# Retention and a GELU layer on one core: a hand-written order of the chunked retention, queries loaded four tokens a partition, and the second layer by seven half-size products

## The chip, the cores and the metric

The kernel runs on one core of one Trainium2 chip. The metric is the device time of a launch in microseconds (us), the median of several executions. An execution called fast is one whose time lies within 1.5% of the fastest of its kernel; a single execution on one core has the state "unknown". The executions of the kernel before lay between 359.5 and 362.5 us on all occasions, so a difference of one us between two single executions means nothing.

The engines are written as the profile has them: PE multiplies matrices (PEld loads its weights), DVE, ACT and POOL are the vector, scalar and general engines, SP issues most DMAs.

## The reference, cut to what matters

```python
# q, k, v: [8 batches, 8 heads, 576 tokens, 64], float32
scores = (q @ k.transpose(0, 1, 3, 2)) / sqrt(64)
gamma  = 1.0 - 2.0 ** (-5.0 - arange(8))                 # one decay a head
Dmat   = where(rel >= 0, gamma[:, None, None] ** rel, 0.0)   # rel = query position - key position
attn   = (scores * Dmat) @ v
x      = attn.transpose(0, 2, 1, 3).reshape(4608, 512)
h      = x @ w_in                                        # w_in  [512, 2048]
g      = gelu_tanh(h)
out    = g @ w_out                                       # w_out [2048, 512], out [4608, 512] float32
```

Because the decay is a power, both kernels fold it into q and k (one factor a token and a head), cut a batch into four chunks of 128 tokens and a tail of 64, and carry a 64 x 64 state a head from chunk to chunk. The work of PE is then mostly the two layers.

## The kernel before

The two layers go in 9 blocks of 512 tokens, numbered 0 to 8. In block t the 16 steps `up` are the first layer and the 8 steps `down` the second; between them stand the steps of the attention of batch t+1. Attention of batch 0 comes before block 0. Only PE's order is written by hand. Some lines are joined here, and the comments are added.

```python
    def load_batch(b):                       # 64 floats (256 B) to a piece, for q, k and v alike
        ...
                nc.sync.dma_start(
                    out=t.rearrange("p (h d) -> p h d", d=D),
                    in_=src[b, :, 128 * c : 128 * c + 128, :].rearrange("h s d -> s h d"),
                )
    ...
    def tr_pair(b, p):                       # q and k of two heads are turned on PE, 8 transposes
        ...
        s = sb.tile([128, 1024], F16, tag="qk", name="qk", bufs=6)
        nc.vector.tensor_copy(out=s, in_=t)
    ...
    def state_scan(b):                       # the states are copied by ACT
        ...
                nc.scalar.copy(out=td[r, c, :, r], in_=w[r])
    ...
    def ffn_steps(t):
        def up(fc):
            hp = bank("hp", 2, "hp")
            for ct in range(4):
                nc.tensor.matmul(hp, w_in_sb[:, ct, 128 * fc : 128 * fc + 128],
                                 xT[:, ct, TB * t : TB * t + TB], start=(ct == 0), stop=(ct == 3))
            nc.scalar.activation(out=gT[:, fc, :], in_=hp, func=AF.Gelu_apprx_tanh)
        def down(i, half):                   # 64 matmuls of 512 columns a block
            if half == 0:
                op[i] = bank("att", 6, "op")
            for f in range(8 * half, 8 * half + 8):
                nc.tensor.matmul(op[i], gT[:, f, 128 * i : 128 * i + 128], w_out_sb[:, f, :],
                                 start=(f == 0), stop=(f == NF - 1))
            ...
    slots = {1: 0, 2: 1, 3: 2, 5: 3, 7: 4, 8: 5, 11: 6, 14: 7, 16: 8, 19: 9}
    with tc.manual_schedule(engines={PE}):
        load_batch(0)
        cast_batch(0, {"k": nc.vector, "q": nc.gpsimd, "v": nc.gpsimd})
        for g in range(4):
            load_w_in(g)
        load_batch(1)                        # batch 1 is loaded ahead of w_out
        ...
        for f in range(NF):
            load_w_out(f)
        for f in range(NF):
            cast_w_out(f)
        for t in range(NTB):
            ...
                cast_batch(t + 1, {"k": nc.gpsimd, "q": nc.vector, "v": nc.gpsimd})
                steps = att_steps(t + 1)
            ...
            for i, f in enumerate(ffn_steps(t)):
                f()
                if i in slots and slots[i] < len(steps):
                    steps[slots[i]]()
```

## Time and profile before

| | before |
|---|---|
| median time | 362.1 us (360.08 to 362.14, 3 runs) |
| span of the profiled execution | 358.8 us |
| start of block 1 | 86.9 us |
| length of blocks 1 to 6 | 35.5, 35.1, 35.1, 35.9, 35.5, 35.5 us |
| length of block 7 | 27.6 us |
| start of block 8 to the end | 31.6 us |

The first view is the page of the kernel before: the span, the busy time of each engine, and two rows of digits, where each digit is a fortieth of the span (about 9 us), in tenths.

```profile
span 358.8 us, 6008 instructions
PE 316.4 (88%) x2400; PEld 159.1 (44%) x2400; DVE 125.9 (35%) x269; ACT 161.9 (45%) x303; POOL 70.3 (20%) x101
PE   0176368799999999999999999999999999999995
DMA  9979989994692898598937931100110011011012
```

PE is full from the tenth slice on. Before that PE is not full and the DMA engines are. The same is told in us by the windows view; its columns are the stretch, its length, then busy time and count of PE, PEld, DVE, ACT and POOL, the granted clock of PE, the DMA share, and GB/s.

```profile
0.00:30.00 30.00, 9.39 (x118) 6.62 (x118) 17.59 (x65) 6.06 (x12) 15.39 (x31) 0.96 0.99 220
30.00:57.00 27.00, 16.71 (x138) 8.86 (x139) 10.94 (x22) 11.97 (x22) 7.58 (x10) 0.66 1.00 243
157.50:192.60 35.10, 34.54 (x285) 17.57 (x284) 14.99 (x29) 17.32 (x33) 10.30 (x15) 1.00 0.76 168
```

The last row is block 3: PE is busy 34.5 of 35.1 us, DVE 15.0. The timeline of PE shows the marks of the block structure; its columns are start, length, engine, line, operation, written tile, read tiles, shapes, count, and in brackets the idle time just before and what ended it.

```profile
71.64 1.89 PE L369 MATMUL op<-w_out_sb,gT 128*128 128x512 f16 x8
...
86.90 1.89 PE L355 MATMUL hp<-xT,w_in_sb 128*128 128x512 f16 x8
...
138.41 1.89 PE L355 MATMUL hp<-xT,w_in_sb 128*128 128x512 f16 x8 [0.44 <-ACT gT L361]
```

L355 is `up`, L369 is `down`. Block 0's second layer begins at 71.64 us, block 1 at 86.90, and in a later block PE idles no longer than 0.44 us at a time.

### The profile page before, as it was taken

Reading aid. Unit: us, or ns where it says so; the run is one execution under the profiler, and the core shown is the slowest. Engines: PE = TensorE matmul, PEld = TensorE weight load, DVE = VectorE, ACT = ScalarE, POOL = GpSimd, SP = SyncE. Lnnn points to the kernel's source line nnn. Section 1 sums busy time; section 2 is a strip of 40 time slices with the busy share of each in tenths; the row PEclk is TensorE's granted clock in tenths of the full one; section 3 lists DMA queues with packets and bytes.
Section 4 is the critical chain, followed back from the end, with each engine's and each line's share of the span. In section 5 each row is a group of like instructions: output and inputs, shape, how many; then the busy total and the mean of one; then the engine's idle time right before and its main releaser. Section 6 shows DMA issues by size and latency. Waiting matters only on the chain.

```text
span 358.8 us, 6008 instructions
## 1 busy us (share of the span) xinstructions
PE 316.4 (88%) x2400; PEld 159.1 (44%) x2400; DVE 125.9 (35%) x269; ACT 161.9 (45%) x303; POOL 70.3 (20%) x101
## 2 busy tenths in 40 slices
PE   0176368799999999999999999999999999999995
PEld 0153134344544454455445544554454444444442
DVE  5287238430762174227422771172117200000000
ACT  1037318722682268236723662366236624714721
POOL 8610430342051333232321232000000000000000
PEclk9995669899999999999999999999999999999999
DMA  9979989994692898598937931100110011011012
GB/s 173 205 230 319 224 193 360 219 188 134 144 218 81 194 225 163 127 235 170 194 108 187 216 82 58 58 2 2 58 60 0 2 60 58 0 60 59 0 38 79
DMA packets 122715, 46.52 MB, mean 130 GB/s; under 512 B 113984, under 2 KB 113984, under 8 KB 122688
## 3 DMA queue, kind: packets, MB, share of 16 engines
q1 hardware_dynamic: 122688, 46.15, 55.2%
q8 instruction: 18, 0.29, 0.4%
q14 instruction: 9, 0.07, 0.1%
HBM read 36.70 MB, written 9.44 MB: 129 GB/s over the span
## 4 chain that ended last, share of the span: by engine, by line
PE 67%; ACT 10%; DMA 9%; DVE 7%; SPq 4%; issue 1%; POOL 1%; DVEq 0%; ACTq 0%
PE op L369 35%; PE hp L355 24%; DVE ret L246 4%; ACT gT L361 4%; SPq L118 3%; DMA ld<-in_moe_w_out_dram 3%; DMA ld<-in_q_dram 3%; ACT tbd_128 L281 2%; ACT tbd_130 L281 2%; PE xs L290 2%; DMA ld<-in_moe_w_in_dram 2%; PE xs L308 2%; PE st L221 2%; PE tr L189 2%; DVE ws L278 1%; DMA ld<-in_v_dram 1%
## 5 line engine op out<-in xcount | busy, mean ns | idle before, releaser
L355 PE MATMUL hp<-xT,w_in_sb 128*128 128x512 f16 x576 | 141.6, 388 | 7.7 <-ACT gT L361 7.5
L369 PE MATMUL op<-w_out_sb,gT 128*128 128x512 f16 x576 | 128.1, 379 | 0.0
L361 ACT ACTIVATE gT<-hp 128x512 f16<-128x512 f32 x144 | 85.2, 598 | 58.6 <-PE hp L355 57.9
L355 PEld LDWEIGHTS <-w_in_sb 128*128 128x128 f16 x576 | 54.7, 99 | 68.8 <-issue 16.7
L369 PEld LDWEIGHTS <-gT 128*128 128x128 f16 x576 | 55.6, 98 | 65.3
L377 ACT COPY ost<-op 128x512 f32<-128x512 f32 x36 | 21.1, 586 | 100.9 <-PE op L369 66.0
L246 DVE TENSOR_TENSOR ret<-st,cm 128x512 f16<-128x512 f32 x64 | 40.7, 684 | 49.5 <-PE st L221 49.4
L146 POOL TENSOR_TENSOR ck<-ld,sc 128x512 f16<-128x512 f32 (+1 forms) x35 | 34.8, 997 | 82.2 <-DMA ld<-in_k_dram 60.9
L195 DVE COPY qk<-tr 128x1024 f16<-128x1024 f16 x32 | 21.9, 686 | 56.5 <-PE tr L189 56.5
L146 DVE TENSOR_TENSOR cq<-ld,sc 128x512 f16<-128x512 f32 (+1 forms) x35 | 22.6, 660 | 40.2 <-DMA ld<-in_q_dram 40.2
L142 POOL CAST cv<-ld 128x512 f16<-128x512 f32 (+1 forms) x40 | 23.1, 590 | 67.4 <-DMA ld<-in_v_dram 36.8
L189 PE MATMUL tr<-ident,ck 128*128 128x128 f16 x128 | 14.7, 234 | 23.5 <-DVE ck L146 15.0
L189 PEld LDWEIGHTS <-ck 128*128 128x128 f16 x128 | 10.6, 104 | 31.7 <-DVE ck L146 15.5
L325 ACT CAST xT<-xs 128x512 f16<-128x512 f32 x32 | 17.2, 589 | 5.0 <-PE xs L308 4.9
L189 PE MATMUL tr<-ident,cq 128*128 128x128 f16 x128 | 14.2, 236 | 1.2 <-POOL cq L146 1.0
L281 ACT CAST tbd_128<-ws 64x256 f16<-64x256 f32 x32 | 12.9, 403 | 3.1 <-DVE ws L278 2.6
L281 ACT CAST tbd_130<-ws 64x256 f16<-64x256 f32 x32 | 12.9, 403 | 2.4 <-DVE ws L278 2.0
L171 ACT CAST w_in_sb<-ld 128x512 f16<-128x512 f32 x8 | 5.0, 620 | 19.6 <-DMA ld<-in_moe_w_in_dram 19.5
L290 PE MATMUL xs<-ret,cv 128*64 128x128 f16 x256 | 11.3, 227 | 1.3 <-DVE ret L246 1.0
L278 DVE TENSOR_TENSOR ws<-vs,gt 128x256 f32<-128x256 f32 x24 | 11.8, 492 | 1.4
L221 PE MATMUL st<-qk 64*128 64x128 f16 x256 | 11.9, 226 | 0.3 <-DVE qk L195 0.3
L221 PEld LDWEIGHTS <-qk 64*128 64x128 f16 x256 | 7.6, 98 | 9.8 <-issue 7.4
(56 smaller groups left out, 125.7 us busy)
## 6 DMA issues: line engine op xcount, KB each, us to landing
out_dram<-ost SPq DMA_DIRECT2D x36, 256.0 KB, 2.0
ld<-in_k_dram SPq DMA_DIRECT2D x32, 256.0 KB, 4.8
ld<-in_q_dram SPq DMA_DIRECT2D x32, 256.0 KB, 4.9
ld<-in_v_dram SPq DMA_DIRECT2D x32, 256.0 KB, 4.9
ld<-in_moe_w_in_dram SPq DMA_DIRECT2D x16, 256.0 KB, 6.4
ld<-in_moe_w_out_dram SPq DMA_DIRECT2D x16, 256.0 KB, 6.0
ld<-in_k_dram SPq DMA_DIRECT2D x16, 64.0 KB, 3.3
ld<-in_q_dram SPq DMA_DIRECT2D x16, 64.0 KB, 2.6
```

Source lines behind the costliest of these rows:

```text
L142: eng[key].tensor_copy(out=dst, in_=raw)
L146: eng[key].tensor_tensor(out=dst.rearrange("p (h d) -> p h d", d=D), in0=raw.rearrange("p (h d) -> p h d", d=D), in1=sc[:, s0 : s0 + nh].u ...
L189: nc.tensor.transpose(t[:, 512 * i + 128 * c : 512 * i + 128 * c + 128], a[key][:, 512 * c + 128 * p : 512 * c + 128 * p + 128], ident,)
L195: nc.vector.tensor_copy(out=s, in_=t)
L221: nc.tensor.matmul(st[hl][:, 128 * c : 128 * c + 128], qk[r, 128 * c : 128 * c + 128], qk[r, 512 + 128 * c : 512 + 128 * c + 128], start=T ...
L246: nc.vector.tensor_tensor(out=r, in0=st[:, 0:w], in1=m.rearrange("p c i -> p (c i)"), op=ALU.mult)
L281: nc.scalar.copy(out=td[r, c, :, r], in_=w[r])
L290: nc.tensor.matmul(x[64 * hl : 64 * hl + 64, 128 * c : 128 * c + 128], a["v"][:, col(c, p, hl)], a["ret", p, hl][:, 128 * c : 128 * c + 12 ...
L355: nc.tensor.matmul(hp, w_in_sb[:, ct, 128 * fc : 128 * fc + 128], xT[:, ct, TB * t : TB * t + TB], start=(ct == 0), stop=(ct == 3),)
L361: nc.scalar.activation(out=gT[:, fc, :], in_=hp, func=AF.Gelu_apprx_tanh)
L369: nc.tensor.matmul(op[i], gT[:, f, 128 * i : 128 * i + 128], w_out_sb[:, f, :], start=(f == 0), stop=(f == NF - 1),)
L377: nc.scalar.copy(out=o, in_=op[i])
```

## The change

The intent was threefold. First, less work on PE: the second layer of blocks 1 to 8 becomes seven products of sums of blocks (112 matmuls of 256 columns in place of 64 of 512), and the transposes of q and k for batches 4 to 7 go to the DMA engines. Second, a shorter opening: q is loaded four tokens to a partition, in pieces of 1 KB in place of 256 B, and both weights are loaded before batch 1. Third, the order of every engine, not of PE alone, is written by hand. The sums of weights that the seven products need are made once, on POOL and DVE: half of them in the second layer of block 0, half in block 1. The sums of activations are made in every block by DVE.

The diff, cut to its core (`...` marks cuts, the comments are added; the loads, the decay factors, the chunked attention and the order of the opening are rewritten too):

```diff
+    elif key == "q":                        # 4 tokens a partition: 1 KB pieces
+            nc.sync.dma_start(
+                out=t.rearrange("p (h x) -> p h x", h=2),
+                in_=src[b, 2 * c : 2 * c + 2, 0:M0, :].rearrange("h (p j) d -> p h (j d)", j=QT),
+            )
...
+    seq += [("i", g, ct) for g in range(4) for ct in range(4)]     # w_in, then w_out, then batches 1 to 7
+    seq += [("o", f) for f in range(NF)]
+    for b in range(1, B):
...
+    def weight_sums(f):
+        s = slice(f, f + 2)
+        d, w = (sb.tile([128, 2, HD], F32, tag=n, name=n, bufs=b) for n, b in (("wd", 2), ("we", 1)))
+        nc.vector.tensor_tensor(out=wt["1"][:, s], in0=W12[:, s], in1=W11[:, s], op=ALU.subtract)
+        nc.gpsimd.tensor_tensor(out=d, in0=W22[:, s], in1=W12[:, s], op=ALU.subtract)
+        nc.gpsimd.tensor_tensor(out=wt["2"][:, s], in0=d, in1=W11[:, s], op=ALU.add)
+        nc.gpsimd.tensor_tensor(out=w, in0=W21[:, s], in1=W11[:, s], op=ALU.subtract)
+        nc.gpsimd.tensor_tensor(out=wt["4"][:, s], in0=w, in1=d, op=ALU.subtract)
...
+    def act_sums(t, f0, f1):                # 4 calls a block
+        nc.vector.tensor_tensor(out=s["1"], in0=a21, in1=a22, op=ALU.add)
+        nc.vector.tensor_tensor(out=s["2"], in0=s["1"], in1=a11, op=ALU.subtract)
+        nc.vector.tensor_tensor(out=a21, in0=a11, in1=a21, op=ALU.subtract)
+        nc.vector.tensor_tensor(out=s["4"], in0=a12, in1=s["2"], op=ALU.subtract)
...
+    def prod(t, m, u):                      # m: one of 7 products, u: one of 2 halves
+        for f in range(NH):
+            nc.tensor.matmul(
+                op[tag][:, HD * u : HD * u + HD], lhs(f), rhs[:, f],
+                start=(new and u == 0 and f == 0), stop=(f == NH - 1), skip_group_check=True,
+            )
...
+    at(0, 2, lambda: turn_pe(1, "q", 0, 8, A.copy))      # block 0, steps 2 and 4 of its second layer
+    at(0, 4, lambda: turn_pe(1, "q", 8, 8, V.tensor_copy))
...
+    for n in range(4):
+        at(*((0, 30), (0, 32), (1, 3), (1, 6))[n], lambda n=n: weight_sums(2 * n))
+        at(1, (1, 2, 12, 14)[n], lambda n=n: weight_copy(2 * n))
+    for b in range(2, B):
...
+        if b == 2:
+            t0, eng = 1, {"k": V, "q": P, "v": A}
+        elif b == 3:                         # batch 3's casts stand in block 1 as well
+            ut = [9, 10, 11, 12] + [14, 15, 16, 17, 18, 19, 20, 21] + [22, 22, 22]
+            t0, eng = 1, {"k": P, "q": P, "v": A}
...
+        if b >= NPE:                         # NPE = 4: batches 4 to 7
+            at(t0, ut[-1] + 1, lambda b=b: turn_dma(b))
...
+        slots = {2: (6, 10, 15, 19, 25)}.get(b, (1, 7, 12, 19, 25))
...
-        def down(i, half):
-            ...
-                    gT[:, f, 128 * i : 128 * i + 128],
-                    w_out_sb[:, f, :],
```

`at(t, u, f)` puts work after step u of block t, on every engine.

## The prediction

> **What bounds the kernel now.** Three parts, from the timeline of PE.
>
> 1. Opening, 0 to 86.9 us, where the second block of 512 tokens starts. Loads rule it: the windows show DMA busy 0.99 (0–30 us) and 1.00 (30–57 us), PE busy only 9.4 and 16.7 us there. Loads in 256 B pieces (q, k, v) move 173–205 GB/s, the 2 KB pieces of the weights 319–360. [...] w_out is loaded behind batch 1 and lands near 62 us, so block 0's second layer starts only at 71.6 us.
> 2. Blocks 1 to 6 with attention of the next batch: 35.5 us each, PE-bound. 128 matmuls of 512 columns at 216 ns (13.8 us for 64, chain of waits) are 27.65 us; attention is the other 7.8 us: 36 transposes at 56 ns = 2.0 us, scores 1.4, states 0.6, value products 1.3, state products 0.8, the rest waits (for GELU 7.5 us in the whole run).
> 3. Blocks 7 and 8 without attention: 27.65 us each, PE-bound, then 3.8 us of last copy and store.
>
> **What the change does.**
>
> - Second layer of blocks 1–8: 112 matmuls of 256 columns in place of 64 of 512. At 216/2 plus about 1 ns (an estimate; transposes with their own weight loads hold 56 ns for 128), 12.2 us for 13.8: −1.6 us a block, −12.7 us, all on PE and so on the path. Added: 16 DVE sums of activations (about 0.4 us each) and five adds of products (0.65): 10 us a block on an engine busy 15 of 34. Not on the path.
> - Batches 4–7: transposes of q and k leave PE for DMA: −2.0 us a block, and −1 us more from a finer interleaving. The moved 1.2 MB must land within some 12 steps (about 13 us). [...] At 200 GB/s they take 6 us: hidden.
> - State copies move from ACT to DVE, casts to POOL and ACT. Attention per block: about 7.0 us for batches 2 and 3, 4.9 for 4–7, in place of 7.8: −13 us over six blocks.
> - Opening: q in 1 KB pieces (3 us a batch instead of 5.5), weights both before batch 1. Batch 0 landed by 19 us, w_in 31, w_out 43, batch 1 60, then 3–4 us of attention: block 1 starts near 64 us instead of 86.9: −23 us.
> - Fillers, sums of weights on POOL (17 us, needed near 84 us): no time.
>
> Sum: 64 + 2×33.3 + 4×31.2 + 2×26.2 + 3.7 = 311.5 span, plus 3.3 (362.1 against the profile's 358.8), plus 1–2 us new waits: **316 us, 308 to 329** (8 in 10). Chances: faster by over 2% 0.97, within 0.02, slower 0.01.
>
> **What would show it.** In the timeline of PE: block 1 starts at 61–68 us; blocks 3–6 last 31 us and blocks 1–2 33; blocks 7–8 26.2; product matmuls 109 ns start to start. DMA share 0.9 or more until 60 us. DVE about 22 us a block, still below PE.
>
> **What would make it wrong.** Transposes by DMA slower than their window, or their issue holding ACT so that GELU and then PE wait; 256-column matmuls not holding 109 ns; DVE late with sums or with the adds that free the product banks; three attention banks too few, so that PE waits for DVE; opening gated by POOL's 16 weight casts rather than by DMA.

No term of the sum went with them: it stays at 311.5 us of span and 316 us of time. Three figures in it are estimates. The 3 us for a batch's queries: four loads of 256 KB are 1.05 MB, 2.9 us at the 360 GB/s that the page before shows for the pieces of 2 KB; no 1 KB piece was in that trace. In the trace after, the windows 60:62 and 62:64, in which batch 2's queries load and its keys and values begin, show 291 and 297 GB/s. The 200 GB/s for the transposes by DMA is what the page before shows for loads in 256 B pieces; what the transposes took is told under e11. The 0.4 and 0.65 us of DVE's additions and adds of products came out as 0.42 to 0.43 us where POOL did not slow them, and as 0.687.

## The result, and the profile after

The kernel after takes 344.07 us (median of 4 runs, 343.66 to 344.59), the one before beside it 361.63 (360.08 to 362.14, 4 runs). The ratio of the two is 0.9531, with a 95% interval from 0.9503 to 0.9559. A ratio is the mean time of one kernel's fast runs over that of the other's of the same rounds, so it is not quite the ratio of the medians. The direction was right. The size was not: 17.6 us came in place of 46, and the time lies above the range of 308 to 329.

```profile
span 342.3 us, 6651 instructions
PE 310.2 (91%) x2660; PEld 189.1 (55%) x2660; DVE 213.1 (62%) x437; ACT 170.9 (50%) x274; POOL 108.8 (32%) x129
PE   5869849994697999999999999999999999999995
DVE  7751644879978467757976677467546752442432
POOL 7748234999920460039224404100000000000000
PEclk9999969997889999999999999999999999999999
```

In the tenth and eleventh slice (77 to 94 us) PE is down to 4 and 6 tenths and its clock to 7 and 8, while DVE and POOL are both full. That is block 1, as the windows show beside the loading of the weights and a later block:

```profile
25.00:40.00 15.00, 14.55 (x78) 6.42 (x78) 5.41 (x11) 9.03 (x17) 9.72 (x14) 1.00 1.02 368
71.50:104.00 32.50, 24.08 (x184) 11.85 (x181) 28.30 (x39) 16.44 (x29) 24.21 (x21) 0.84 0.69 157
154.60:187.40 32.80, 32.12 (x299) 20.31 (x297) 25.35 (x46) 17.70 (x28) 15.94 (x17) 1.00 0.84 194
```

In the second row DVE is busy 28.3 us for 39 instructions (0.73 us each); in the third, 25.4 us for 46 (0.55 each). The waits of PE in block 1, from its timeline:

```profile
71.45 2.79 PE L390 MATMUL hp<-xT,w_in_sb 128*128 128x512 f16 x12
...
83.52 0.61 PE L289 MATMUL st<-tq,tk 64*128 64x128 f16 x8 [4.70 <-DVE tk L254]
...
84.42 4.78 PE L390 MATMUL hp<-xT,w_in_sb 128*128 128x512 f16 x12
...
93.95 0.40 PE L289 MATMUL st<-tq,tk 64*128 64x128 f16 x8 [3.21 <-DVE tk L254]
...
94.52 4.45 PE L390 MATMUL hp<-xT,w_in_sb 128*128 128x512 f16 x12
```

PE waits 4.70 and 3.21 us for DVE's copy of the turned keys (`tk`), and after each wait the same 12 matmuls that took 2.79 us at 71.45 take 4.78 and 4.45. The granted clock of this stretch is 0.84 (second row of the windows), so here each of the two waits costs its own length and 2.0 or 1.7 us more. The length of a wait alone does not tell: after one of 2.28 us 12 matmuls took 4.45 us (e13_mended3), and after one of 2.79 us they took 2.76 (e11_all_pe_turns), as in stretches with a clock of 1.00. What sets the clock was not shown. With three smaller waits the waits of block 1 are 9.9 us; the slow stretches add about 4.0 (2.0 and 1.7 for the two rows of 12, the rest from the small groups between them, an estimate from the same timeline).

Blocks 3 to 6 and the products look like this. In the first fence are two rows of PE from block 3 and one of ACT; in the second, products of block 7.

```profile
168.15 1.29 ACT L377 CAST xT<-xs 128x512 f16<-128x512 f32 x1
168.41 0.40 PE L289 MATMUL st<-tq,tk 64*128 64x128 f16 x8
169.49 0.32 PE L309 MATMUL us<-cv,ck 128*64 128x64 f16 x8 [0.68 <-ACT xT L377]
```

```profile
299.61 1.91 PE L466 MATMUL opA<-w_out_sb,gT 128*128 128x256 f16 x16
301.36 1.91 PE L466 MATMUL opB<-wt,s 128*128 128x256 f16 x16
```

Sixteen product matmuls start 1.75 us apart, so 109 ns each, as predicted. The wait of 0.68 us recurs in each of blocks 3 to 6: PE wants a bank which ACT's copy of the attention output has not yet freed.

Where the time went, by stage of the span:

| stage | before | predicted | after | after − before | after − predicted |
|---|---|---|---|---|---|
| start of block 1 | 86.90 | 64 | 71.45 | −15.45 | +7.45 |
| block 1 | 35.47 | 33.3 | 49.46 | +13.99 | +16.16 |
| block 2 | 35.12 | 33.3 | 33.65 | −1.47 | +0.35 |
| blocks 3 to 6, sum | 142.06 | 124.8 | 131.21 | −10.85 | +6.41 |
| block 7 | 27.62 | 26.2 | 26.07 | −1.55 | −0.13 |
| block 8 and end | 31.63 | 29.9 | 30.46 | −1.17 | +0.56 |
| span | 358.8 | 311.5 | 342.3 | −16.5 | +30.8 |

Three rows carry the miss of 30.8 us in the span: block 1 with half of it, the opening, and blocks 3 to 6. The predicted time had another 3.3 us between the span and the time, where 1.9 were found, and 1 to 2 us for new waits, which are in the rows here.

### The profile page after: what moved, and what is told of

Same layout as the page of the kernel before. It is cut to its first block, busy times and chain, and to the rows that moved or that the text cites. A ratio compares the mean times of both kernels' runs of the same rounds, so it can differ in the third digit from the quotient of the medians.

```text
span 342.3 us, 6651 instructions
## 1 busy us (share of the span) xinstructions
PE 310.2 (91%) x2660; PEld 189.1 (55%) x2660; DVE 213.1 (62%) x437; ACT 170.9 (50%) x274; POOL 108.8 (32%) x129
## 4 chain that ended last, share of the span: by engine, by line
PE 72%; DMA 8%; DVE 8%; SPq 5%; ACT 4%; issue 1%; POOL 1%; DVEq 0%
PE hp L390 30%; PE opB L466 12%; PE opC L466 9%; PE opA L466 8%; PE op L408 3%; DMA ld<-in_moe_w_in_dram 3%; DMA ld<-in_moe_w_out_dram 3%; PE xs L338 3%; SPq L90 3%; PE st L289 2%; PE xs L356 2%; ACT xT L377 2%; PE us L309 2%; DMA ld<-in_q_dram 2%; SPq L78 1%
## 5 line engine op out<-in xcount | busy, mean ns | idle before, releaser
L377 ACT CAST xT<-xs 128x512 f16<-128x512 f32 x31 | 40.1, 1294 | 29.5 <-PE xs L356 22.6
L223 POOL TENSOR_TENSOR cq<-ld,sc 128x512 f16<-128x512 f32 x28 | 31.6, 1155 | 46.0 <-DMA tq<-cq 21.0
L232 POOL TENSOR_TENSOR ck<-ld,sc 128x512 f16<-128x512 f32 x27 | 28.9, 1089 | 37.3 <-PE us L309 29.6
L466 PEld LDWEIGHTS <-s 128*128 128x128 f16 x384 | 36.5, 98 | 4.9
L466 PE MATMUL opA<-w_out_sb,gT 128*128 128x256 f16 x256 | 30.9, 273 | 0.0
L329 DVE CAST tbd<-ws 64x256 f16<-64x256 f32 x48 | 20.6, 430 | 1.2
L408 PE MATMUL op<-w_out_sb,gT 128*128 128x512 f16 x64 | 17.7, 396 | 0.5 <-ACT ost L413 0.5
L219 ACT CAST cv<-ld 128x512 f16<-128x512 f32 x28 | 17.5, 628 | 1.1 <-DMA ld<-in_v_dram 1.1
L466 PE MATMUL opB<-wt,gT 128*128 128x256 f16 x128 | 16.4, 273 | 0.5 <-DVE ost L480 0.5
L449 DVE TENSOR_TENSOR s<-s,gT 128x512 f16<-128x512 f16 x32 | 15.9, 498 | 1.1
```

What stands on the lines that cost most here:

```text
L223: eng.tensor_tensor(out=dst.rearrange("p (j l d) -> p l j d", j=QT, l=2), in0=raw.rearrange("p (l j d) -> p l j d", l=2, j=QT), in1=sc[:, ...
L232: eng.tensor_tensor(out=dst.rearrange("p (h d) -> p h d", d=D), in0=raw.rearrange("p (h d) -> p h d", d=D), in1=sc[:, s0 : s0 + nh].unsque ...
L329: cp(out=td[r, c, :, r], in_=w[r])
L377: nc.scalar.copy(out=xT[:, g0 : g0 + 2].rearrange("p g n (i j) -> p g n j i", j=QT), in_=src)
L408: nc.tensor.matmul(op[i], gT[t][:, f, i], w_out_sb[:, f, :], start=(f == 0), stop=(f == NF - 1))
L466: nc.tensor.matmul(op[tag][:, HD * u : HD * u + HD], lhs(f), rhs[:, f], start=(new and u == 0 and f == 0), stop=(f == NH - 1), skip_group_ ...
```

## The experiments

Thirteen kernels ran. Those of one look are single executions (state unknown) and are read by their blocks. The first four were compared with one run of the kernel before on the same chip, 360.58 us, those named e5 to e8 with one of 359.91, and e11 with six fast ones (median 360.9). e9, e10, e12 and e13 were timed (four fast executions each, the median is given); their blocks, as those of the kernel after, are from one profiled execution of 342.38, 335.29, 333.95, 330.62 and 344.22 us.

| run | us | start of block 1 | block 1 | block 2 | blocks 3 to 6, typical |
|---|---|---|---|---|---|
| after | 344.07 | 71.45 | 49.46 | 33.65 | 32.80 |
| e1_no_sums | 338.03 | 70.92 | 43.81 | 33.65 | 32.80 |
| e2_memsets | 340.54 | 72.27 | 44.95 | 33.65 | 32.80 |
| e3_late_q | 344.70 | 70.09 | 51.14 | 33.65 | 32.80 |
| e4_plain | 353.80 | 73.88 | 40.05 | 35.93 | 35.27 |
| e5_early_sums | 342.35 | 77.11 | 41.95 | 33.65 | 32.80 |
| e6_keys_act | 346.58 | 71.07 | 47.75 | 36.11 | 32.80 |
| e7_slots | 341.75 | 72.18 | 49.01 | 33.12 | 32.26 |
| e8_before_split | 362.16 | 85.76 | 35.75 | 35.98 | 35.42 |
| e9_combined | 344.69 | 75.99 | 43.17 | 35.82 | 32.25 |
| e10_mended | 333.58 | 75.16 | 38.96 | 33.98 | 32.26 |
| e11_all_pe_turns | 351.09 | 73.10 | 47.69 | 34.55 | 34.55 |
| e12_mended2 | 333.99 | 67.43 | 46.14 | 33.13 | 32.26 |
| e13_mended3 | 329.74 | 67.30 | 42.16 | 33.98 | 32.26 |

The theory of the first runs for block 1: while POOL reads its operands, DVE's additions with two inputs in SBUF wait for it. DVE's instructions stand in the written order in the trace, so the cast and the copy of the keys behind the additions come late, PE waits for the keys, and its clock falls (to 0.84 over the stretch). The rival: DVE simply has too much to do in block 1, whatever POOL does.

The ground for the theory is how DVE's and POOL's timelines of the kernel after lie together (DVE's rows, then POOL's):

```profile
77.62 1.26 DVE L449 TENSOR_TENSOR s<-s,gT 128x512 f16<-128x512 f16 x1
78.80 1.48 DVE L450 TENSOR_TENSOR gT<-gT 128x512 f16<-128x512 f16 x1
80.20 1.37 DVE L451 TENSOR_TENSOR s<-gT,s 128x512 f16<-128x512 f16 x1
...
85.99 1.79 DVE L329 CAST tbd<-ws 64x256 f16<-64x256 f32 x2
...
96.49 0.59 DVE L329 CAST tbd<-ws 64x256 f16<-64x256 f32 x2
...
97.57 0.43 DVE L449 TENSOR_TENSOR s<-s,gT 128x512 f16<-128x512 f16 x1
```

```profile
77.26 1.33 POOL L432 TENSOR_TENSOR we<-w_out_sb 128x512 f32<-128x512 f16 x1
78.68 1.32 POOL L433 TENSOR_TENSOR wt<-we,wd 128x512 f16<-128x512 f32 x1
79.96 1.33 POOL L430 TENSOR_TENSOR wd<-w_out_sb 128x512 f32<-128x512 f16 x1
```

The addition of L449 takes 0.43 us at 97.57, alone, and 1.26 at 77.62. Each of the three long additions ends 0.28 to 0.29 us after the POOL instruction that ran when it began (78.88 after 78.59, 80.28 after 80.00, 81.57 after 81.29): in these three cases DVE's addition lasted until a POOL instruction had ended. The masking of the scores has one input in PSUM, and its mean is 684 ns before and 685 after. The state copies (`tbd`), which the change moved from ACT to DVE, have one input, in SBUF, and are held up too: two of them take 1.79 us at 85.99, beside POOL's casts, and 0.59 at 96.49, with POOL idle.

### e1_no_sums: POOL's sums of weights left out (wrong result)

```diff
-        nc.gpsimd.tensor_tensor(out=d, in0=W22[:, s], in1=W12[:, s], op=ALU.subtract)
-        (and the three other POOL sums)
+    (wt["2"], wt["4"] set once to 0.02; weight_copy copies wt["1"])
```

> The 16 sums of weights on POOL are left out (constants in their place, so the result is wrong on purpose); casts, DVE work and PE order stay. Theory, POOL's work on SBUF holds up DVE in block 1: the adds of activations on DVE in block 1 fall from 1.2-1.5 us to 0.42-0.6, the waits of PE for the key copies (4.7 and 3.2 us) go to under 1 us each, block 1 lasts 34-37 us instead of 49.5, the run about 330-333 instead of 344. Rival, DVE simply has more work of its own in block 1 than it can do: nothing changes, 343-345.

Measured: 338.03 us; block 1 43.81 us in place of 49.46; the first wait for `tk` 0.41 us in place of 4.70. The second stayed:

```profile
86.85 0.61 PE L289 MATMUL st<-tq,tk 64*128 64x128 f16 x8 [3.28 <-DVE tk L254]
```

So the sums of weights cost 5.65 us of block 1, about a third of its 16 us over the prediction, and the run missed its expectation. For the first wait the rival is out, since DVE does the same instructions here. In the same trace DVE's four additions took 0.42 us each from 76 to 78 us, with POOL idle; from 81 to 86, where POOL cast batch 3's queries, two state copies took 1.89 us in place of 0.59 and two of the four additions 1.16 and 1.27. POOL has more than one job in block 1, and the second one did what the first had done.

### e2_memsets: as many POOL instructions, which only write (wrong result)

```diff
-        (the four POOL sums)
+        w = sb.tile([128, 1200], F32, tag="we", name="we", bufs=1)
+        for _ in range(4):
+            nc.gpsimd.memset(w, 0.0)
```

> As e1, but POOL stays as busy as in the changed kernel: in the place of each sum a memset of a scratch tile that takes about the same 1.25 us and reads nothing. Theory, DVE waits only for POOL operations that read SBUF: as e1, 330-333. Rival, any POOL operation holds DVE up, or POOL's full queue delays the casts behind it: block 1 stays near 49 us and the run near 344.

Measured: 340.54 us, block 1 44.95 us, waits for `tk` 0.40 and 4.98: neither the 330 to 333 of the theory nor the 49 us block of the rival. One trace holds both cases. POOL's rows come first, then DVE's:

```profile
73.32 9.18 POOL L431 MEMSET we<- 128x1200 f32 x8
82.47 4.55 POOL L223 TENSOR_TENSOR cq<-ld,sc 128x512 f16<-128x512 f32 x4
```

```profile
77.94 0.42 DVE L446 TENSOR_TENSOR s<-s,gT 128x512 f16<-128x512 f16 x1
...
84.94 1.16 DVE L446 TENSOR_TENSOR s<-s,gT 128x512 f16<-128x512 f16 x1
```

Beside memsets the same line takes 0.42 us, beside the casts 1.16. In this trace a busy POOL did not slow the additions by itself (0.42 to 0.43 us for the four beside memsets); a POOL that reads SBUF did (1.16 to 1.27 for the four beside the casts). By what the two get in each other's way was not shown. The second wait is longer than in e1 (4.98 us for 3.28): POOL reaches batch 3's casts only after the memsets, and all four additions fall beside them.

### e3_late_q: batch 1's queries turned later in block 0

The kernel after has its other long wait in the opening (PE's timeline):

```profile
47.05 0.61 PE L248 MATMUL tr<-ident,cq 128*128 128x128 f16 x4 [5.16 <-DVE cq L223]
```

Step 2 of block 0's second layer puts transposes of batch 1's queries in front of matmuls, some of whose weights had already landed.

```diff
-    at(0, 2, lambda: turn_pe(1, "q", 0, 8, A.copy))
-    at(0, 4, lambda: turn_pe(1, "q", 8, 8, V.tensor_copy))
+    at(0, 14, lambda: turn_pe(1, "q", 0, 8, A.copy))
+    at(0, 15, lambda: turn_pe(1, "q", 8, 8, V.tensor_copy))
...
-        u = 7 + 5 * c
+        u = 17 + 3 * c
```

> Only the order in block 0: the transposes of batch 1's queries come after the first 14 steps of the second layer instead of after 2, and the rest of batch 1's attention follows later and closer. Theory, PE's own order made it wait 5.2 us for a query load while matmuls whose weights had landed stood behind it: that wait falls to under 1 us, block 1 starts at 65-67 us instead of 71.5, the run about 338-340. Rival, loads alone set the start of block 1: the wait moves to later waits for keys, and block 1 still starts at 71.

Measured: 344.70 us, outside the expectation. The wait of 5.16 us is gone and block 1 starts only 1.4 us earlier, at 70.09: what the rival said of the wait came true. Waits of 2.25 us (for the cast of the key tail) and 1.43 us (for the attention output) stand in its place, so the tail of batch 1 takes over as the limit. Over the runs whose opening was not edited the start lies between 70.9 and 73.9 us, so 1.4 us is within the scatter. Mending the order of the queries alone does not give the opening back.

### e4_plain: second layer by whole matmuls, everything else of the change kept

```diff
-            for m in (1, 6, 5, 7, 2, 3, 4):
-                for u in range(2):
-                    steps.append(lambda m=m, u=u: (prod(t, m, u), after(t, m, u)))
+            for i0, tags in ((0, "AB"), (2, "CA")):
+                for f in range(0, NF, 2):
+                    steps.append(lambda f=f, i0=i0, tags=tags: (
+                        [down_mm(t, i0 + n, f + e, tags[n]) for e in range(2) for n in range(2)],))
+                steps.append(lambda i0=i0: store_pair(t, i0, (A.copy, V.tensor_copy)))
```

(act_sums and weight_sums are left out too.)

> Second layer of all blocks by plain 512-column matmuls; no sums of weights or activations; attention, order and transposes as in the change. Prediction's sizes: blocks 3 to 6 get 1.6 us longer (34.4), blocks 7 and 8 27.7. Theory: block 1 loses its waits and lasts 34-37 us, so the run is near 341-344: the half-size products with their sums bring nothing in all, because block 1 gives back what blocks 2 to 8 gain.

Measured: 353.80 us, slower than the expectation. Block 1 takes 40.05 us, but each of blocks 2 to 6 takes 2.3 to 2.5 us more: in blocks 3 to 6 about 1.75 for the larger matmuls and 0.7 for a new wait for ACT's copy of the output. Two things follow. The seven products are worth some 9.7 us on the whole even as they stand (353.80 against 344.07), and in block 1 alone they lose 9.4. And block 1 has no wait for the keys here although POOL still casts batch 3's queries beside it: without DVE's additions POOL's casts alone do no such harm. (This run by itself would fit the rival too, as it takes work from DVE.) Without its waits (2.99 us) block 1 is 37.1 us here, and 1.6 less with products is 35.5. e5's block 1, with the products and a full clock, is 35.6 without its waits (6.3 us). That is the work of PE in block 1, where the prediction had 33.3 for all of it. Part of the gap is a count: it had 36 transposes in each of blocks 1 and 2, and block 1 has 52 (at 56 ns, 0.9 us more), because queries of two batches are turned in it.

### e5_early_sums: all sums of weights on DVE, in f16, in block 0

```diff
-        nc.gpsimd.tensor_tensor(out=d, ...)   # and three more
+        nc.vector.tensor_tensor(out=d, ...)   # and three more, f16
...
-        at(*((0, 30), (0, 32), (1, 3), (1, 6))[n], lambda n=n: weight_sums(2 * n))
+        at(*((0, 3), (0, 5), (0, 11), (0, 16))[n], lambda n=n: weight_sums(2 * n))
```

> The sums of weights run on DVE in f16 during block 0's second layer instead of on POOL from 60 to 85 us; the rest as in the change, result correct. Theory (POOL's reading operations hold DVE up): as the run without sums, block 1 43-45 us and the run 337-340, because the casts of batch 3 on POOL still make PE wait some 3 us once. Rival, the sums cost time wherever they run: 343-345.

Measured: 342.35 us, correct, and missed the expectation. Block 1 fell to 41.95 us, and its start went back to 77.11: the sums stood in DVE's queue before copies that the opening needs (a wait of 3.55 us is new: ACT's copy of an output bank stood behind a state copy that waited 2.96 us for DVE). The cost went to another place in the same queue.

### e6_keys_act: ACT copies the turned keys of batches 2 and 3

```diff
-                    at(b - 1, u - 1, lambda b=b, c=c: turn_pe(b, "k", 4 * c, 4, V.tensor_copy))
+                    at(b - 1, u - 1, lambda b=b, c=c: turn_pe(b, "k", 4 * c, 4, A.copy))
```

(The copy of the tail's keys and queries goes to ACT as well.)

> The sums stay on POOL; only the copies of the transposed keys of batches 2 and 3 go from DVE to ACT. Theory: PE waited because this copy stands in DVE's queue, in order, behind four slowed sums; off that queue the waits of 4.7, 3.2 and 0.7 us go, the granted clock stays at 1.0, block 1 lasts 36-40 us though DVE's sums are still 1.2-1.5 us each, the run 331-336. Rival, DVE is late with everything: the wait moves to the masked scores or to the sums before the products, block 1 stays over 44 us.

Measured: 346.58 us, block 1 47.75 us and block 2 36.11. The rival came true. The wait went from the keys to what DVE does next:

```profile
84.70 0.22 PE L338 MATMUL xs<-ret,cv 128*64 128x128 f16 x1 [2.34 <-DVE ret L298]
```

DVE is late with everything behind the slow additions, the masked scores (`ret`) included. Taking one copy away from it changes which name stands in the brackets.

### e7_slots: one slot of attention moved by a step

```diff
-        slots = {2: (6, 10, 15, 19, 25)}.get(b, (1, 7, 12, 19, 25))
+        slots = {2: (6, 10, 15, 19, 25)}.get(b, (1, 7, 13, 19, 25))
```

> For batches 3 to 7 the scores of the third chunk come one step later (13 instead of 12), so that the three attention banks are asked for 0.86 us later. Theory, the 0.68 us wait a block is for a bank that ACT's strided copy of 1.29 us frees late: it goes to 0, blocks 3 to 6 last 32.1 us instead of 32.8, the run 340.5-342. Rival, a bank is short anywhere: the wait moves to the next chunk and the blocks stay at 32.8.

Measured: 341.75 us, as expected; blocks 3 to 6 took 32.26, 32.26, 32.26 and 32.12 us, and the wait of 0.68 us is gone from all four. ACT's copy of the attention output, which reorders the tokens since the queries lie four to a partition, takes 1.29 us where it took 0.59. Which part of the reordering costs the time was not tried. One step of room hides it. It is the first row here for the kernel after, the second for the one before (groups of instructions; busy time and mean ns after the bar):

```profile
L377 ACT CAST xT<-xs 128x512 f16<-128x512 f32 x31 | 40.1, 1294 | 29.5 <-PE xs L356 22.6
```

```profile
L325 ACT CAST xT<-xs 128x512 f16<-128x512 f32 x32 | 17.2, 589 | 5.0 <-PE xs L308 4.9
```

### e8_before_split: the kernel before, with its attention cut finer

This one measures by itself what finer interleaving costs PE. Work and engines are those of the kernel before.

```diff
-            lambda: (score_pairs(b, (0, 1), False), state_mm(b), state_scan(b)),
+            lambda: score_pairs(b, (0,), False),
+            lambda: score_pairs(b, (1,), False),
+            lambda: (state_mm(b), state_scan(b)),
...
-            lambda: av_pairs(b, (0, 1), True),
+            lambda: av_pairs(b, (0,), True),
+            lambda: av_pairs(b, (1,), False),
...
-            lambda: av_pairs(b, (2, 3), False),
+            lambda: av_pairs(b, (2,), False),
+            lambda: av_pairs(b, (3,), False),
```

> The kernel before, with each batch's attention matmuls cut into three more groups between the layers' matmuls (scores of pairs 0 and 1, values of pairs 0 and 1 and of 2 and 3 apart, states apart from scores). The same matmuls in the same number. Theory, each further group costs PE 0.1-0.2 us at its edges: blocks 2 and 3, without their waits for GELU, get 0.4-0.8 us longer than 34.7, the run 363-366. Rival, grouping is free: within 0.1 us a block.

Measured: 362.16 us, which a single run cannot tell from the kernel before; the blocks met the expectation (0.68 and 0.45 us for blocks 2 and 3). With their waits taken off, blocks 1 to 6 are 35.13, 35.36, 35.13, 35.62, 35.14 and 35.13 us, against 34.62, 34.68, 34.68, 34.87, 34.63 and 34.62 in the kernel before: 0.5 us more a block (four of the six give 0.51, 0.45, 0.51 and 0.51, the others 0.68 and 0.75) for the same work. The count that fits these runs is not groups but changes of shape: how often in a block PE goes from one array mode (`128*128`, `64*128` or `128*64` in the timeline) to another. Counted in the timelines it is 11 in the kernel before, 18 here and 24 in blocks 3 to 6 of the kernel after. So 0.51 us for 7 changes is 0.073 us each, and the 13 more of the kernel after would be 0.95 us a block, an estimate from these numbers. e11 below checks it twice. It puts 36 transposes a block back, which brings 14 more changes from one group of matmuls to another at the same 24 changes of mode. Without waits its blocks are longer by 1.97 us, which is 55 ns a transpose and nothing for the groups. And with as many transposes as the kernel before, they last 34.09 us; some 34.65 of the kernel before less the 1.55 that products save in block 7 is 33.10, so 13 more changes of mode cost 0.99 us, 0.076 each. The runs agree that a change costs something. What is in the 0.073 to 0.076 us was not shown.

### e9_combined: the remedies at once, timed

```diff
 (e5's sums on DVE, at steps 0, 13, 18 and 22 of block 0; e3's later queries, e6's key copies on ACT, e7's slots;)
+    at(1, 1, lambda: turn_tail(1, A.copy))      # the tail of batch 1 goes into block 1
```

> All mends together: sums of weights on DVE in f16 early in block 0, query transposes of batch 1 late in block 0, that batch's 64-token tail moved into block 1 (its tokens are needed first in block 2), key copies of batches 2 and 3 on ACT, third chunk one step later. Theory: block 1 starts at 65-68 us, lasts 36-38 without waits over 1 us, block 2 33.2, blocks 3-6 32.1, blocks 7 and 8 as before: 318-326 us. If the causes overlap more than thought: 327-335.

Measured: 344.69 us (342.38 to 345.71), ratio to before 0.9551 (0.9509 to 0.9594), no better than the change itself and far from the expectation. Block 1 fell to 43.17 us, and the start went to 75.99. Sums of weights stood ahead of batch 1's query copies on DVE, and 3.23 us of waiting for the attention output at the start of block 1 is new. Adding up remedies without asking what each puts at the head of which queue gave nothing.

### e10_mended: POOL's casts spread, batch 3's queries meant to be out of the additions' way, timed

```diff
+            for n in range(4):
+                weight_sums(2 * n)                # DVE, right behind the casts of w_out
...
-            ut = [9, 10, 11, 12] + [14, 15, 16, 17, 18, 19, 20, 21] + [22, 22, 22]
+            ut = [16, 17, 18, 19] + [20, 21, 22, 23, 24, 25, 26, 27] + [28, 28, 28]
 (upper half of w_out cast by ACT; batch 1's queries and batch 2's keys cast by POOL; its key copies on ACT)
```

> What the runs so far suggest, in one kernel: sums of weights on DVE in f16 right behind the last casts of w_out (half of which go to ACT); all query casts of batch 1 on POOL and its query transposes late in block 0; that batch's tail in block 1; batch 2's keys cast on POOL and copied by ACT; all POOL casts of batch 3 and its query transposes moved from the first half of block 1 into its second half, so that no reading POOL operation runs beside the sums of activations there; third chunk a step later. Theory (DVE and its waits for POOL are what block 1 pays for): start of block 1 at 66-68 us, block 1 36-39 us with adds at 0.42 us and clock 1.0, block 2 33-34, blocks 3-6 32.3, run 321-327. Rival (DVE has too much work of its own there): block 1 stays at 42 or more, run 330 or more.

Measured: 333.58 us (332.99 to 335.29), ratio to before 0.9238 (0.9213 to 0.9263). Block 1, in the windows view:

```profile
75.20:114.10 38.90, 36.14 (x364) 23.73 (x364) 25.40 (x51) 26.51 (x49) 16.77 (x18) 1.00 0.88 199
```

DVE does 51 instructions in 25.4 us (0.50 each), and PE's clock is full. This is the shortest block 1 of all that have products: waits of 2.75 us and 36.2 of work, which includes the tail of batch 1. It met the expectation for block 1, where the rival had 42 us or more; but batch 2's key casts and copies were taken from DVE as well. And the move of batch 3's casts did not work as meant. In the trace POOL makes those of the queries from 79.75 to 85.29 us, earlier in the block than in the kernel after (from 85.51, in a block that began at 71.45), in two pairs that each waited for a load; 13 of the 16 additions fell in gaps of POOL (0.41 to 0.55 us), three did not (0.83, 0.83 and 1.15). The run as a whole missed 321 to 327. The opening paid for block 1, as the 20 sums stood in front of batch 1's first key cast:

```profile
58.27 0.61 PE L248 MATMUL tr<-ident,ck 128*128 128x128 f16 x4 [6.56 <-DVE ck L232]
```

### e11_all_pe_turns: no transposes by DMA

```diff
-    NPE = 4
+    NPE = 8
```

> The change with its transposes by DMA undone: batches 4 to 7 turn queries and keys on PE as batches 2 and 3 do. Prediction's size: blocks 3 to 5 get 36 transposes of 56 ns more, 2.0 us, and wait no more than now; the run 351-354. Rival, the new copies out of PSUM on DVE bring waits as in block 1: 3 us a block or more.

Measured: 351.09 us, at the edge of the expectation. Blocks 3 to 5 take 34.55 us with a wait of 0.46, against 32.80 with a wait of 0.68: 1.97 us of PE a block, as predicted (2.0), of which 1.75 show in the block's length. In the kernel after the transposes by DMA land in time; the table of DMA issues gives their median to landing:

```profile
tk<-ck ACTq DMA_TRANSPOSE x4, 4.9
tq<-cq ACTq DMA_TRANSPOSE x4, 6.4
```

From issue to landing 0.59 MB took 4.9 and 6.4 us (medians), beside loads of 256 KB of the attention's inputs that took 4.7 to 5.7. No run moved the same bytes both ways, so whether such a transfer is as fast as a load was not shown.

### e12_mended2: e10 with half of the sums of weights later, timed

```diff
-            for n in range(4):
+            for n in range(2):
                 weight_sums(2 * n)
+    at(0, 33, lambda: weight_sums(4))
+    at(1, 1, lambda: weight_sums(6))
...
-            cc(1, "k", c, V if c == 0 else P)
+            cc(1, "k", c, P)
```

> e10_mended with its own mistake taken out: there the first key cast of batch 1 stood in DVE's queue behind 20 sums and PE waited 6.6 us for it. Now that cast is on POOL, two of the four groups of sums stay at the start of block 0's second layer, one goes to its end and one to the start of block 1, where DVE was idle for 3.9 us. Theory: that wait falls under 1.5 us, block 1 starts at 67-69 us and lasts 38-40, run 325-329. If loads set the start of block 1 after all, it stays at 71 or later and the run at 329-332.

Measured: 333.99 us (331.18 to 334.64), ratio 0.9221 (0.9167 to 0.9275). The wait of 6.56 us is gone and block 1 starts at 67.43 us, but it takes 46.14: ACT stood 3.95 us waiting for DVE, which was in slowed sums, so GELU was late, PE waited 3.70 us for it, and the clock fell (0.89 from 71.5 to 104 us):

```profile
71.76 0.82 ACT L329 CAST tbd<-ws 64x256 f16<-64x256 f32 x2 [3.95 <-DVE ws L326]
...
73.25 1.86 PE L390 MATMUL hp<-xT,w_in_sb 128*128 128x512 f16 x4 [3.70 <-ACT gT L396]
```

### e13_mended3: e12 with those sums off ACT's path, timed

```diff
-    at(0, 33, lambda: weight_sums(4))
-    at(1, 1, lambda: weight_sums(6))
+    at(1, 0, lambda: weight_sums(4))
+    at(1, 5, lambda: weight_sums(6))
...
-    at(0, 33, lambda: scan(1, NC - 1, A.copy))
+    at(0, 33, lambda: scan(1, NC - 1, V.tensor_copy))
```

> e12_mended2 started block 1 at 67.4 us as expected, but block 1 then lasted 46.1: a state copy on ACT waited 4 us for DVE, which was in a group of slowed weight sums, and four GELUs stood behind that copy in ACT's queue. Here that last state copy goes to DVE and the two late groups of sums come after it, at steps 0 and 5 of block 1; nothing else changes. Theory (the whole excess of block 1 is in-order queues behind DVE): the 3.7 us wait goes, the clock stays up, block 1 lasts 37-40 us, run 325-329. Rival (something in block 1 itself, such as the amount of DVE work, keeps it above 42 us whenever it starts early): 331 or more.

Measured: 329.74 us (327.55 to 330.81), correct, ratio to before 0.911 (0.9055 to 0.9164). It beats the kernel before and the kernel after. Block 1 starts at 67.30 us and takes 42.16, of which 4.28 are waits, some 1.7 the slow clock after one of them, and 36.2 work, as in e10. The run's time lies between the two expectations. The wait and the slow stretch behind it:

```profile
85.19 0.32 PE L309 MATMUL us<-cv,ck 128*64 128x64 f16 x8 [2.28 <-DVE ret L298]
85.44 4.45 PE L390 MATMUL hp<-xT,w_in_sb 128*128 128x512 f16 x12
```

At that time POOL is at batch 3's query casts again (from 81.82 us, four in 4.66 us), and two additions of activations take 1.28 us each. So the early start is kept, and block 1 is again longer than e10's 38.96, with the same collision in it. Whether both can be had together stays open.

## Why the prediction was wrong, point by point

**The step that failed first: "Fillers, sums of weights on POOL (17 us, needed near 84 us): no time."** The durations were not the trouble: 16 sums of 1.15 to 1.60 us, 20.5 in all where 17 were predicted, on an engine with room. What was wrong is that POOL's time was taken as nobody else's. Beside POOL instructions that read SBUF, an addition of DVE took up to 1.48 us in place of 0.42 (e2_memsets has both cases in one trace, 1.16 and 0.42), and two state copies up to 1.89 in place of 0.59. So eight of the 16 additions of activations in block 1 (0.78 to 1.48 us), a pair of state copies (1.79) and two key casts (1.63 and 1.52 for 0.69) were slow, what stood behind them in DVE's queue came late, and PE with it. Block 1 took 49.46 us in place of 33.3. Its 16.2 us are 9.9 of waits, about 4.0 of slow clock, and about 2.2 of work that was miscounted (35.5 in place of 33.3, from e4_plain and e5_early_sums). Leaving the sums of weights out gives back only 5.65 (e1_no_sums). The second long wait comes from the same collision with another job of POOL, batch 3's query casts, which the prediction had put down, in one line with the state copies that now go to DVE, as "casts to POOL and ACT" with no cost either. How much of the smaller waits is due to it was not taken apart.

**"DVE … 10 us a block on an engine busy 15 of 34. Not on the path."** Right for blocks 3 to 6, where DVE is busy 20 to 25 us in 32.8 and the list of PE's waits has none for it. Wrong for block 1. DVE is busy 28.3 of the first 32.5 us there, and an engine with room on the average can still be on the path for some us, because its instructions follow the written order, and a slow one in front holds what PE needs next. e6_keys_act showed this by moving the wait from the keys (4.70 us in the kernel after) to the scores (2.34). The prediction named "DVE late with sums" among its dangers, and gave it no time.

**"−1 us more from a finer interleaving."** It went the other way. Blocks 3 to 6 took 32.8 us in place of 31.2: 0.68 is a wait for ACT's copy (e7_slots takes it away by one step), and about 0.95 is the price of 13 more changes of PE's array mode in a block, an estimate from e8_before_split that e11_all_pe_turns bears out (0.99). The prediction read the shares of small matmuls off the trace of before and did not see that they had been cheap because they stood together (cut finer, the same work takes 0.5 us a block more in e8_before_split).

**"Block 1 starts near 64 us."** It started at 71.45. The loading part was right: the last piece of batch 1 landed at 60.3 us (predicted 60), and the weights moved at 368 GB/s with a DMA share of 1.02. "Then 3–4 us of attention" was wrong: PE was 11.2 us from there. About 4.7 of these were attention, 0.8 a wait, and 5.6 were 26 of the 64 matmuls of block 0's second layer (216 ns each), which the prediction left out. PE was behind with them after the wait of 5.16 us that came from the hand-written order, and a granted clock of 0.80 from 43 to 60 us. Without that wait others come from the casts and copies of batch 1's tail. e3_late_q shows that removing the first wait alone moves the start by no more than the scatter. e12_mended2 and e13_mended3 start at 67.3 to 67.4, with the tail moved into block 1 and the casts shared out anew; which of these edits gave how much was not taken apart.

**Right.** The product matmuls hold 109 ns, and block 7 went from 27.62 to 26.07 us, 1.55 for the predicted 1.6. The transposes by DMA are hidden and worth 1.97 us of PE a block for the predicted 2.0 (e11_all_pe_turns). The last two blocks were right to 0.43 us. Block 2 was right to 0.35, but by luck: it has 20 transposes in place of the 36 that were counted, since batch 3's queries are turned in block 1. With 36 it takes 34.55 us (e11_all_pe_turns), 1.25 over the prediction, much as blocks 3 to 6. The prediction missed because of the stretch in which all parts of the change meet, and because of the finer interleaving, not because of the cost of a single matmul, load or addition by itself.

## What to carry to other kernels

Before calling work on POOL free, list the DVE instructions that run beside it and read SBUF twice, and the copies from SBUF to SBUF: in these traces each of them could last until the POOL instruction that it met had ended (an addition up to 1.48 us in place of 0.42, two state copies up to 1.89 in place of 0.59), and what stands behind it in DVE's queue is late too. When work is cut finer to be laid between large matmuls, count the changes of PE's array mode (0.073 to 0.076 us each here, an estimate), and price them from a trace where the same work is cut coarser. A remedy that moves work to another queue has to be checked at the new place, since in e3, e5, e6, e9, e10 and e12 the wait came back under another name.
